# Where PSUM is emptied: 35 reads of PSUM move from VectorE to ScalarE in an adaLN attention and MLP block, with one addition on GpSimd

## The chip, the core and the metric

One core of a Trainium2 chip runs the whole program. The metric is the device time of one execution in microseconds (us); less is better. The engines are called as the profile calls them: PE is TensorE (PEld its weight loads), DVE is VectorE, ACT is ScalarE, POOL is GpSimd, SP is the queue that issues the transfers. Each engine works through its own instructions in the order in which the program lists them.

## What is computed

A transformer block with adaptive layer norm, on 2048 rows of 512 numbers in float32: attention with 32 heads of 16 and a single key and value head, then an MLP of width 1376. The reference, cut to what matters:

```
mod = (silu(c) @ w_mod)                      # six rows: sa, ca, ga, sb, cb, gb
h = layernorm(x) * (1 + ca) + sa
q = h @ wq ; k = h @ wk ; v = h @ wv         # 32 heads for q, one for k and v
p = softmax(q k^T * 16 ** -0.5) ; o = p v
x = x + ga * (o @ wo)
h = layernorm(x) * (1 + cb) + sb
x = x + gb * (gelu(h @ w1 + b1) @ w2 + b2)   # the output
```

## The kernel before

**Units and steps.** The rows are cut into 8 blocks of 256, the heads into 8 groups of 4. A unit is one block with one group (64 units), and it goes over the 2048 keys in 8 steps of 256 keys. The kernel writes all instructions in an order of its own, so each engine's order is what the Python code emits.

**What a step does.** `sexp` makes four products `e` of keys and queries (L589, 64 rows of the array each, 512 columns) and four exponentials from them into `p` (L590, on ACT). `pv` multiplies the `p` of an earlier step with the values (L601, `acc`). `Max.step` makes products `m` for a unit that comes later (L509), from each of which DVE takes the maximum (L514, `mx`). In most steps there is also half of a *batch*: a few products of the other work (query projections `qps`, output projection `wops`, transposes `tp`, first MLP layer `w1ps`, second MLP layer `w2ps`), given out in generators by `batches` and cut in two halves of 64 array rows (L184), one for each of two neighbouring steps. What a generator does behind its last product runs when the second half has been issued (`go_on_`, which calls `resume`).

**PSUM.** The products `e` rotate over three banks, `m` over three, `acc` has one, and all batches share a single bank with the tag `x`. Where two steps hold the halves of a batch, the second one's four `e` take the banks 0, 1, 2 and 0, and when the next step holds a new batch its first `e` takes bank 0 again:

```python
groups = [mixture(maxes(1, n // 2, 0.0), exps(1, [(X, 0, 0), (X, 1, 1), (Y, 0, 2)])),
          halves(batch, 0) + exps(0, [(X, 0, 0)])]
...
issue(mixture(maxes(0, n // 2, 0.0, reduces), exps(0, [(X, 1, 0), (Y, 0, 1), (Y, 1, 2)])),
      halves(batch, 1) + [(0.0, go_on_)] + exps(1, [(Y, 1, 0)]))
```

The last number in each triple is the bank. `go_on_` stands ahead of the step's fourth exponential, so whatever it puts on ACT stands there too.

**The three places that the change touches.** `qproj_late` copies a query sum out of PSUM (L442) and lets POOL split it in a high and a low part; it runs 14 times, early. `modulate` copies the first of two transposed pairs of a block (L862), for POOL to scale; it does so in the 7 blocks whose flag `fast` is not set. `store` adds `x1` to a sum of the second MLP layer (L967) and sends the rows out; there are two sums per block, 14 in those 7 blocks. The eighth block (`fast`, at the end) keeps its code. `later(n, ...)` puts a call off by n ticks of the schedule's clock; two steps take four ticks.

Of the kernel before, what the change touches and what calls it, by code (L numbers as in the profile page):

```python
# [11 lines left out]
ALU = mybir.AluOpType  # L12
# [36 lines left out]
def adaln_mqa_mlp(  # L49
# [15 lines left out]
    nc = tc.nc  # L65
# [60 lines left out]
    def split(dst_h, dst_l, src, eng_h, eng_l, between=None):  # L126
        if eng_h is nc.gpsimd:
            eng_h.tensor_scalar(out=dst_h, in0=src, scalar1=1.0, scalar2=0.0, op0=ALU.mult, op1=ALU.add)
        elif eng_h is nc.scalar:
            eng_h.copy(dst_h, src)  # L130
        else:
            eng_h.tensor_copy(out=dst_h, in_=src)
        if between:
            between()
        eng_l.tensor_tensor(out=dst_l, in0=src, in1=raw(dst_h), op=ALU.subtract)  # L135
# [7 lines left out]
    def later(n, fn):  # L143
        if draining[0]:
            fn()
        else:
            pending.append((clock[0] + n, fn))
# [17 lines left out]
    def batches(ps, pairs, size, ready=lambda n: True, begin=True, end=True):  # L165

        todo = [(a, b_) for wh, wl, xh, xl in pairs for a, b_ in ((wh, xh), (wl, xh), (wh, xl))]
        last = len(todo) - 1
        parts = -(-len(todo) // size)
        for i in range(parts):  # L170
            part = range(i * len(todo) // parts, (i + 1) * len(todo) // parts)
            while not ready(part[-1] // 3):
                yield -1
            yield [(ps, *todo[n], begin and n == 0, end and n == last) for n in part]
# [230 lines left out]
    def send_q(b, g, qH, qL):  # L405
        for t, src in enumerate((qH, qL)):
            nc.sync.dma_start(out=dq[b][g][t].rearrange("a r j n -> (a r j) n"), in_=raw(src))
        state["q"] -= 1
        sent.add((b, g))
# [3 lines left out]
    def qpairs(b, g):  # L413
        hH, hL = hts[b]
        gs = slice(g * P, (g + 1) * P)
        return [(wqH[:, k, gs], wqL[:, k, gs], hH[:, k, :], hL[:, k, :]) for k in range(KD)]

    def qtiles(b, g):
        qH = att.tile([P, BQ], F32R, name=f"qH{b}_{g}", tag="xH", bufs=2)
        qL = att.tile([P, BQ], F32R, name=f"qL{b}_{g}", tag="xL", bufs=2)  # L420
        return qH, qL
# [16 lines left out]
    def qproj_late(b, g):  # L438
        ps = psum.tile([P, BQ], F32, name=f"qps{b}_{g}", tag="x")
        yield from batches(ps, qpairs(b, g), BATCH)  # L440
        q32 = wts_pool["rest"].tile([P, BQ], F32, name=f"q32_{b}_{g}", tag="ot", bufs=2)
        nc.vector.tensor_copy(out=q32, in_=ps)  # L442
        qH, qL = qtiles(b, g)
        split(qH, qL, q32, nc.gpsimd, nc.gpsimd)
        later(4, lambda: send_q(b, g, qH, qL))
# [334 lines left out]
    def rest_steps(b, fast, rp, bank, ons, ready):  # L780
# [4 lines left out]
        for hf in range(w // HQ):  # L785
# [5 lines left out]
            x1, w1ts = early[b]  # L791
# [38 lines left out]
            for t in range(2):  # L830
                ps = psum.tile([P, D], F32, name=f"wops{b}_{hf}_{t}", **bank())
# [27 lines left out]
            def modulate(dp, ps):  # L859
                if not fast and dp == 0:  # L860
                    src = rp.tile([P, 2, HQ], F32, name=f"tc{b}_{hf}", tag="ot", bufs=2)
                    nc.vector.tensor_copy(out=src, in_=ps)  # L862
                for d2 in range(2):
                    d = 2 * dp + d2
                    h32 = rp.tile([P, HQ], F32, name=f"h322_{b}_{hf}_{d}", tag="h322", bufs=2)
                    if fast or dp:
                        nc.scalar.activation(h32, ps[:, d2, :], AF.Identity, scale=cb1[:, d:d + 1], bias=sb[:, d:d + 1])
                    else:
                        nc.gpsimd.tensor_scalar(out=h32, in0=src[:, d2, :], scalar1=cb1[:, d:d + 1], scalar2=sb[:, d:d + 1],
                                                op0=ALU.mult, op1=ALU.add)  # L870
                    if fast:
                        split(hH[:, d, :], hL[:, d, :], h32, nc.vector, nc.gpsimd if d2 else nc.vector)
                    else:
                        split(hH[:, d, :], hL[:, d, :], h32, nc.gpsimd, nc.gpsimd)
# [6 lines left out]
            if fast:  # L881
                tps = [psum.tile([P, 2, HQ], F32, name=f"tp2_{b}_{hf}_{dp}", **bank()) for dp in range(KD // 2)]
                for t in range(2):
                    for dp in range(KD // 2):
                        turn2(dp, tps[dp], t)
                    stir(STIR[t])
                for dp in range(KD // 2):
                    modulate(dp, tps[dp])
                for t in range(2):
                    add_bias(t)  # L890
                yield MOD_WAIT
            else:
                for dp in range(KD // 2):
                    ps = psum.tile([P, 2, HQ], F32, name=f"tp2_{b}_{hf}_{dp}", **bank())
                    yield [(ps[:, d2, t * P:(t + 1) * P], xh[:, t, (2 * dp + d2) * P:(2 * dp + d2 + 1) * P], ident,
                            t + d2 == 0, t + d2 == 2) for t in range(2) for d2 in range(2)]
                    modulate(dp, ps)
                yield 4
# [50 lines left out]
            for f in range(GROUP if fast else 0, NF):  # L949
# [3 lines left out]
                ps = psum.tile([P, HQ], F32, name=f"w1ps{b}_{hf}_{f}", **bank())  # L953
# [10 lines left out]
            def store(t, ps, cols=slice(0, D)):  # L964
                row = row0 + hf * HQ + t * P
                ot = rp.tile([P, D], F32, name=f"ot{b}_{hf}_{t}", tag="ot", bufs=2)
                nc.vector.tensor_tensor(out=ot[:, cols], in0=ps[:, :cols.stop - cols.start], in1=x1[:, t, cols], op=ALU.add)  # L967
                send = lambda: nc.sync.dma_start(out=of[row:row + P, cols], in_=ot[:, cols])
                if fast:
                    send()  # L970
                else:
                    later(2, send)

            while weights:
                yield 2
            for t in range(2):
                sl = slice(t * P, (t + 1) * P)
                for cols in (slice(0, D), ):
                    place = dict(tag="m", bufs=3) if b == len(blocks) - 2 and t else bank()
                    ps = psum.tile([P, D], F32, name=f"w2ps{b}_{hf}_{t}_{cols.start}", **place)  # L980
                    ops = [(gH[:, f, sl], gL[:, f, sl], w2H[:, f, cols], w2L[:, f, cols]) for f in range(NF)]
                    yield from batches(ps[:, :cols.stop - cols.start], ops, BATCH, lambda f: made.issuperset(range(f + 1)))
                    if fast:
                        later(1, lambda t=t, ps=ps, cols=cols: store(t, ps, cols))
                        yield 2
                    else:
                        store(t, ps)
# [158 lines left out]

    draining[0] = True
    late = [qproj_late(b, g) for b in range(2) for g in range(KD)]
    projections = [qproj(b, g) for b in range(2) for g in range(KD)]

# [105 lines left out]
    mod_state["rows"] = wts_pool["rest"].tile([P, D], F32, name="modl_sb", tag="x1", bufs=2)  # L1256
    nc.scalar.copy(mod_state["rows"], mod_state["ps"])
    put_off(*late, late_mods(), *[qproj_late(b, g) for b in range(2, NB) for g in range(KD)])

    steps = [NKT * blocks[b][1] // BQ for b, _ in units]  # L1260
# [169 lines left out]
```

## Time and profile before

| what | value |
|---|---|
| time, median of 3 runs | 1600.91 us (1600.77 to 1601.91) |
| profiled execution: its own time | 1599.49 us |
| profiled execution: span from first to last instruction | 1597.6 us |
| granted TensorE clock, mean over the span | 0.996 of full speed |
| PE busy | 1560.3 us, 98% |
| DVE busy | 1412.9 us, 88%, 2473 instructions |
| ACT busy | 1203.0 us, 75%, 2393 instructions |
| POOL busy | 666.1 us, 42%, 1176 instructions |

The profile is one execution. Busy time is the union of an engine's instructions, and PE's products overlap each other, so a PE that is busy all the time may still be waiting for something between two products; the chain of work that ended last and the order of single instructions tell more.

### The profile page before, as it was taken

What the parts mean: (1) busy time and instruction counts of PE and PEld (TensorE: products, weight loads), DVE (VectorE), ACT (ScalarE), POOL (GpSimd) and SP (SyncE); (2) the same over time, 40 slices, a digit from 0 to 9 for tenths busy, and PEclk for the clock granted to TensorE, in tenths of its full rate; (3) what the DMA queues carried; (4) which work ended last, traced back from release to release, by engine and by line L of the source; (5) the groups of instructions that cost most, each with busy time, mean ns of one, the idle gap of its engine ahead of it and who ended that gap; (6) DMA issues with size and microseconds to landing.
All of it is one profiled execution on the core that took longest, in us unless ns stands there. A gap on an engine that the chain in (4) does not pass through costs nothing.

```text
span 1597.6 us, 41064 instructions
## 1 busy us (share of the span) xinstructions
PE 1560.3 (98%) x16369; PEld 1006.3 (63%) x16369; DVE 1412.9 (88%) x2473; ACT 1203.0 (75%) x2393; POOL 666.1 (42%) x1176
## 2 busy tenths in 40 slices
PE   5999999999999999999999999999999999999998
PEld 3466665557665676657665676656666576656667
DVE  6899999899999998999989999999999999999715
ACT  5577778778777887778877887778877787778853
POOL 4445344747422571246413462234602474225711
PEclk8999999999999999999999999999999999999999
DMA  7136312313022220303112120213112130122232
GB/s 257 73 109 205 117 68 71 125 32 107 17 63 65 68 68 25 103 17 106 32 44 84 53 85 22 78 42 98 42 35 91 42 98 18 62 72 64 80 132 74
DMA packets 79285, 121.59 MB, mean 76 GB/s; under 512 B 15774, under 2 KB 52382, under 8 KB 78836
## 3 DMA queue, kind: packets, MB, share of 16 engines
q1 hardware_dynamic: 79076, 118.95, 23.2%
q8 instruction: 128, 2.10, 0.6%
q14 instruction: 65, 0.53, 0.1%
q10 hardware_dynamic: 16, 0.00, 0.0%
HBM read 91.13 MB, written 27.27 MB: 74 GB/s over the span
## 4 chain that ended last, share of the span: by engine, by line
PE 90%; DVE 6%; DMA 2%; POOL 1%; SPq 1%; ACT 0%; issue 0%; DVEq 0%; POOLq 0%
PE acc L601 30%; PE m L509 22%; PE e L589 17%; PE w1ps L184 8%; DVE mx L514 5%; PE w2ps L184 4%; PE wops L184 2%; PE qps L184 1%; PE w2ps L178 1%; DMA xt<-in_A_x_dram 1%; PE w1ps L178 1%; PE tp L184 1%; PE kps L160 1%; DMA qst<-dq 1%; DVE st L807 0%; DMA os<-drs 0%
## 5 line engine op out<-in xcount | busy, mean ns | idle before, releaser
L514 DVE TENSOR_REDUCE mx<-m 128x1 f32<-128x512 f32 x2048 | 1271.4, 682 | 107.6 <-PE m L509 81.3
L590 ACT ACTIVATE p<-e 128x512 f32<-128x512 f32 x2048 | 1069.4, 599 | 311.1 <-PE e L589 233.2
L509 PE MATMUL m<-ks,qst 64*128 64x512 f32 x2048 | 823.9, 425 | 17.4 <-DVE mx L514 11.0
L589 PE MATMUL e<-qst,ks 64*128 64x512 f32 x2048 | 739.1, 409 | 2.8 <-ACT p L590 1.5
L601 PE MATMUL acc<-p,va 128*32 128x256 f32 x8192 | 550.5, 386 | 0.6 <-DMA qst<-dq 0.6
L509 PEld LDWEIGHTS m<-ks,qst 64*128 64x128 f32 x2048 | 364.1, 184 | 185.8 <-DVE mx L514 157.0
L589 PEld LDWEIGHTS e<-qst,ks 64*128 64x128 f32 x2048 | 366.6, 185 | 85.2 <-ACT p L590 59.5
L601 PEld LDWEIGHTS acc<-p,va 128*32 128x32 f32 x8192 | 214.9, 109 | 220.6 <-issue 115.7
L184 PE MATMUL w1ps<-h2H,w1t 64*128 64x256 f32 x1232 | 236.3, 288 | 0.0
L558 POOL TENSOR_SCALAR mt<-turned 8x32 f32<-8x32 f32 x256 | 53.2, 208 | 362.4 <-DVE turned L564 350.4
L184 PEld LDWEIGHTS w1ps<-h2H,w1t 64*128 64x128 f32 x1232 | 184.2, 185 | 31.7 <-issue 23.0
L184 PE MATMUL w1ps<-h2L,w1t 64*128 64x256 f32 x616 | 169.4, 275 | 0.0
L184 PE MATMUL w2ps<-w2H,gH 64*128 64x512 f32 x286 | 118.1, 413 | 0.0
L184 PE MATMUL w2ps<-w2L,gH 64*128 64x512 f32 x286 | 117.4, 411 | 0.0
L184 PE MATMUL w2ps<-w2H,gL 64*128 64x512 f32 x286 | 117.4, 410 | 0.0
L184 PEld LDWEIGHTS w1ps<-h2L,w1t 64*128 64x128 f32 x616 | 113.8, 185 | 0.0
L920 POOL TENSOR_SCALAR tt<-tt 128x256 f32<-128x256 f32 x77 | 31.1, 404 | 162.8 <-ACT tt L919 162.8
L744 POOL TENSOR_TENSOR os<-os 128x256 f32<-128x256 f32 x28 | 20.6, 734 | 100.9 <-DMA os<-drs 100.2
L921 POOL TENSOR_TENSOR tt<-tt,z 128x256 f32<-128x256 f32 x77 | 57.1, 741 | 6.4
L135 POOL TENSOR_TENSOR gL<-z,gH 128x256 fp32r<-128x256 f32 x77 | 56.8, 738 | 6.4
L931 POOL TENSOR_TENSOR z<-tt,z 128x256 f32<-128x256 f32 x77 | 56.5, 733 | 6.0
L930 POOL TENSOR_TENSOR tt<-tt,z 128x256 f32<-128x256 f32 x77 | 56.7, 736 | 0.0
(188 smaller groups left out, 1498.2 us busy)
## 6 DMA issues: line engine op xcount, KB each, us to landing
w1t<-dw SPq DMA_DIRECT2D x82, 512.0 KB
qst<-dq SPq DMA_DIRECT2D x128, 64.0 KB
do<-oc SPq DMA_DIRECT2D x64, 128.0 KB
dw<-w1s SPq DMA_DIRECT2D x11, 512.0 KB
xt<-in_A_x_dram SPq DMA_DIRECT2D x4, 1024.0 KB
dq<-qH SPq DMA_DIRECT2D x16, 256.0 KB
dq<-qL SPq DMA_DIRECT2D x16, 256.0 KB
qst<-dq SPq DMA_DIRECT2D x128, 32.0 KB
```

Of the source, the lines that this page charges most:

```text
L135: eng_l.tensor_tensor(out=dst_l, in0=src, in1=raw(dst_h), op=ALU.subtract)
L178: nc.tensor.matmul(ps, a, b_, start=first_, stop=last_)
L184: nc.tensor.matmul(ps, a[rows], b_[rows], start=first_ and s == 0, stop=last_ and s == 1)
L509: nc.tensor.matmul(m, qsts[u][rows, j, t * P:(t + 1) * P], ks[rows, kc * 512:(kc + 1) * 512], start=True, stop=True)
L514: nc.vector.tensor_reduce(out=self.mx[u][:, i, kc:kc + 1], in_=m, axis=AX.X, op=ALU.max)
L558: nc.gpsimd.tensor_scalar(out=mt[:, g:g + 32], in0=turned[g:g + 4 * T, :], scalar1=1.0, scalar2=0.0, op0=ALU.mult, op1=ALU.add)
L589: nc.tensor.matmul(e, ks[rows, kt * P:(kt + 1) * P], rhs, start=True, stop=True)
L590: nc.scalar.activation(ptiles[u, K][:, j, s, :], e, AF.Exp, scale=0.25)
L601: ins = nc.tensor.matmul(accs[u][32 * cidx:32 * cidx + 32, :], va[:, kt, :], rhs, start=kt == 0, stop=kt == NKT - 1)
L921: nc.gpsimd.tensor_tensor(out=tt, in0=tt, in1=z, op=ALU.mult)
L930: nc.gpsimd.tensor_tensor(out=tt, in0=tt, in1=z, op=ALU.mult)
L931: nc.gpsimd.tensor_tensor(out=z, in0=tt, in1=z, op=ALU.add)
```

## The change

In `qproj_late` and `modulate` the copy out of PSUM is issued on ACT in place of DVE. In `store` the addition that read PSUM becomes a copy on ACT and, one tick later, an addition in place on POOL; the rows are sent after four ticks in place of two. The last block's `store` is as before.

```diff
@@ qproj_late
         q32 = wts_pool["rest"].tile([P, BQ], F32, name=f"q32_{b}_{g}", tag="ot", bufs=2)
-        nc.vector.tensor_copy(out=q32, in_=ps)
+        nc.scalar.copy(q32, ps)
         qH, qL = qtiles(b, g)
@@ modulate
                 if not fast and dp == 0:
                     src = rp.tile([P, 2, HQ], F32, name=f"tc{b}_{hf}", tag="ot", bufs=2)
-                    nc.vector.tensor_copy(out=src, in_=ps)
+                    nc.scalar.copy(src, ps)
@@ store
                 ot = rp.tile([P, D], F32, name=f"ot{b}_{hf}_{t}", tag="ot", bufs=2)
-                nc.vector.tensor_tensor(out=ot[:, cols], in0=ps[:, :cols.stop - cols.start], in1=x1[:, t, cols], op=ALU.add)
                 send = lambda: nc.sync.dma_start(out=of[row:row + P, cols], in_=ot[:, cols])
                 if fast:
+                    nc.vector.tensor_tensor(out=ot[:, cols], in0=ps[:, :cols.stop - cols.start], in1=x1[:, t, cols], op=ALU.add)
                     send()
                 else:
-                    later(2, send)
+                    nc.scalar.copy(ot[:, cols], ps[:, :cols.stop - cols.start])
+                    later(1, lambda: nc.gpsimd.tensor_tensor(out=ot[:, cols], in0=ot[:, cols], in1=x1[:, t, cols], op=ALU.add))
+                    later(4, send)
```

On ACT, at the end of the first block's first sum of the second MLP layer (`p_7` and `e_7` belong to the last step of a unit, `p_0` and `e_0` to the first step of the next one; in `e_7_1_1` the numbers are step, key half and array half):

```order
 L590 ACTIVATE p_7_6678<-e_7_0_0_6708 128x512
 L590 ACTIVATE p_7_6678<-e_7_1_0_6716 128x512
+L972 COPY ot_0_0_6719<-w2ps_0_0_0_6207 128x512
 L590 ACTIVATE p_7_6678<-e_7_1_1_6723 128x512
 L590 ACTIVATE p_0_6742<-e_0_0_1_6743 128x512
```

The copy stands between the third and the fourth exponential of the step; the other 31 copies that have a batch behind them stand in the same position.

On DVE, at the same place, the instruction that goes:

```order
 L514 TENSOR_REDUCE mx_6483<-m_1_0_0_0_6696 128x1
 L514 TENSOR_REDUCE mx_6483<-m_1_0_1_0_6704 128x1
-L967 TENSOR_TENSOR ot_0_0_6719<-w2ps_0_0_0_6207,x_0_4235 128x512
 L514 TENSOR_REDUCE mx_6483<-m_1_0_2_0_6712 128x1
 L514 TENSOR_REDUCE mx_6483<-m_1_0_3_0_6726 128x1
```

The two maxima behind it stand directly behind the two ahead of it now.

On PE, the first products of the step behind that copy, with what each waits for; first before:

```order
L601 MATMUL acc_6474<-p_6_6659,va 32x256 x3
L184 MATMUL w2ps_0_1_0_6721<-w2H,gH_0_5023 128x512 [waits DVE_49]
L509 MATMUL m_1_1_0_1_6739<-ks,qst_159 128x512
L589 MATMUL e_0_0_1_6743<-qst_158,ks 128x512 [waits Activation_49]
L509 MATMUL m_1_1_1_1_6746<-ks,qst_159 128x512 [waits DVE_49]
```

and with the change:

```order
L601 MATMUL acc_6474<-p_6_6659,va 32x256 x3
L184 MATMUL w2ps_0_1_0_6721<-w2H,gH_0_5023 128x512 [waits Activation_49]
L509 MATMUL m_1_1_0_1_6739<-ks,qst_159 128x512 [waits DVE_49]
L589 MATMUL e_0_0_1_6743<-qst_158,ks 128x512 [waits Activation_49]
L509 MATMUL m_1_1_1_1_6746<-ks,qst_159 128x512 [waits DVE_49]
```

The order is the same. The new batch's first product, which needs bank `x`, waits for ACT in place of DVE, and the step's first `e`, which needs bank 0, waits for ACT in both: for the exponential of `e_7_1_1`.

## Rows read from the trace of the kernel before

**Rows 1.** The page, busy time of each engine (share of the span) and instructions.

```profile
PE 1560.3 (98%) x16369; PEld 1006.3 (63%) x16369; DVE 1412.9 (88%) x2473; ACT 1203.0 (75%) x2393; POOL 666.1 (42%) x1176
```

**Rows 2.** The page, the chain that ended last: shares of the span by engine.

```profile
PE 90%; DVE 6%; DMA 2%; POOL 1%; SPq 1%; ACT 0%; issue 0%; DVEq 0%; POOLq 0%
```

**Rows 3.** The chain in order of time, 440 to 448.5 us: start, us, what.

```profile
444.44 1.00 PE acc L601 x16
447.28 1.01 PE acc L601 x16
```

**Rows 4.** The chain in order of time around the last query copy.

```profile
243.73 1.27 DVE mx L514 x2
245.04 0.69 DVE q L442
245.74 1.21 DVE mx L514 x2
```

**Rows 5.** Lines and tiles: count, duration in ns (min/median/max), first and last start.

```profile
L442 DVE COPY q<-qps x14: 690/692/692, 95.5 to 245.0; 128x512 f32<-128x512 f32 x14
L862 DVE COPY tc<-tp x7: 679/682/682, 335.3 to 1436.2; 128x512 f32<-128x512 f32 x7
L967 DVE TENSOR_TENSOR ot<-w2ps,x x16: 683/692/692, 444.2 to 1593.9; 128x512 f32<-128x512 f32 x16
L433 ACT COPY q<-qps x1: 585/585/585, 70.8 to 70.8; 128x512 f32<-128x512 f32 x1
```

**Rows 6.** Timeline around the w2ps sum that ends at 444.2: start, us, engine, instruction.

```profile
444.76 0.59 ACT L590 ACTIVATE p<-e 128x512 f32<-128x512 f32 x1
...
444.37 1.07 PE L601 MATMUL acc<-p,va 128*32 128x256 f32 x16
...
445.36 0.18 PEld L184 LDWEIGHTS w2ps<-w2H,gH 64*128 64x128 f32 x1 [0.41 <-DVE ot L967]
...
445.48 0.19 PEld L589 LDWEIGHTS e<-qst,ks 64*128 64x128 f32 x1
...
445.70 0.39 PE L589 MATMUL e<-qst,ks 64*128 64x512 f32 x1
...
446.13 2.07 ACT L590 ACTIVATE p<-e 128x512 f32<-128x512 f32 x4 [0.78 <-PE e L589]
```

**Rows 7.** Timeline, the same places after a query copy and a transposed-pair copy.

```profile
106.94 1.08 ACT L590 ACTIVATE p<-e 128x512 f32<-128x512 f32 x2
...
108.14 0.19 PEld L589 LDWEIGHTS e<-qst,ks 64*128 64x128 f32 x1
...
519.36 0.62 ACT L590 ACTIVATE p<-e 128x512 f32<-128x512 f32 x1
...
520.11 0.19 PEld L589 LDWEIGHTS e<-qst,ks 64*128 64x128 f32 x1
```

**Rows 8.** Timeline after two ACT instructions `h` of the second transposed pair.

```profile
525.05 1.04 ACT L867 ACTIVATE h<-tp,sb,cb 128x256 f32<-128x256 f32 x2
...
525.95 0.62 ACT L590 ACTIVATE p<-e 128x512 f32<-128x512 f32 x1
...
526.62 0.49 PE L589 MATMUL e<-qst,ks 64*128 64x512 f32 x1 [0.21 <-ACT p L590]
```

**Rows 9.** Timeline, weight loads later in the step of group 6.

```profile
446.78 0.18 PEld L509 LDWEIGHTS m<-ks,qst 64*128 64x128 f32 x1 [0.19 <-DVE mx L514]
446.78 0.18 PEld L589 LDWEIGHTS e<-qst,ks 64*128 64x128 f32 x1
```

**Rows 10.** Groups by line, form kept apart: busy us, mean ns, idle before.

```profile
L823 POOL TENSOR_TENSOR x<-x,b2g 128x512 f32<-128x512 f32 x16 | 20.1, 1278 | 0.0
```

**Rows 11.** Timeline near the end, around the seventh block's second sum.

```profile
1560.52 0.68 DVE L967 TENSOR_TENSOR ot<-w2ps,x 128x512 f32<-128x512 f32 x1
1561.49 1.02 ACT L867 ACTIVATE h<-tp,sb,cb 128x256 f32<-128x256 f32 x2 [7.41 <-PE tp L879]
```

## The prediction

> **What bounds the kernel now.** I read the page first, then the chain that ended last, then single instructions around the places of the change. The page has PE busy all the time, DVE for 88% and ACT for 75% [rows 1], which invites taking work from DVE. The chain says something else: 90% of the span lies on PE, 6% on DVE, 0% on ACT [rows 2]. In order of time the chain runs from one `acc` to the next at a steady pace, 444.44 to 447.28, which is 2.84 us for a step [rows 3]; DVE comes into it in short pieces only. Of the 35 instructions that leave DVE, one is in the chain: the last query copy, 0.69 us at 245.04 between maxima [rows 4]. So on DVE there is next to nothing to win.
>
> The step of 2.84 us is then looked at for what it waits for. At the end of a step that closes a batch, ACT's fourth exponential runs from 444.76 to 445.35; PE works at `acc` meanwhile, begins the next step with weights at 445.36, and loads the weights of that step's first `e` at 445.48 [rows 6]. This `e` goes into bank 0, which the fourth exponential has just read. The load comes 0.13 us after the exponential's end. It comes 0.12 us after it behind a query copy (106.94 + 1.08 = 108.02, then 108.14) and 0.13 us behind a transposed-pair copy (519.36 + 0.62 = 519.98, then 520.11) [rows 7]; I looked at all 32 such places, and they lie between 0.11 and 0.13 us. How close can it come? Where a first `e` on bank 0 was held in earnest, by an exponential that ended at 525.95 + 0.62 = 526.57, it went at 526.62, 0.05 us later [rows 8]. That leaves 0.06 to 0.08 us of room. ACT is idle for 0.78 us in each step [rows 6], but that idle time lies behind the fourth exponential and ahead of the next step's first one: it waits for this very `e`.
>
> **What is removed.** From DVE: 14 query copies of 0.692, 7 pair copies of 0.682 and 14 of the 16 additions of 0.692 [rows 5], together 24.2 us of DVE's time. What they hold up: the maxima behind them, and through the three `m` banks PE's next `m`. After the addition at 444.24 an `m` does wait for a maximum, 0.19 us until 446.78, but the `e` beside it starts at 446.78 too [rows 9], and that one is set by ACT: the step's first exponential began at 446.13, one takes 0.60 (0.59 and 0.62 in rows 6 and 7), so it ended at 446.73. Taking the DVE part away leaves the step as it is. I cost the removal at 0. The bounds are a gain of 0.69 us, the copy in the chain, and, if those waits for `m` were what counts, 32 x 0.19 = 6.1 us; I take 0 since PE is the one in the chain there [rows 3].
>
> **What is added on ACT.** 35 copies of 128 x 512 out of PSUM. The trace has one on ACT, 0.585 us [rows 5]. Four exponentials of 0.60 in a row took 2.07 us [rows 6], so each behind the first adds (2.07 - 0.60) / 3 = 0.49, 0.11 less than it lasts; a copy among them adds about 0.585 - 0.11 = 0.48. Its data are there in time, since the batch's last product is issued ahead of the third exponential's. The copy stands ahead of the fourth exponential, as the order of ACT in the section on the change shows. So that one ends at 445.35 + 0.48 = 445.83, and the next step's first `e` can load weights at 445.83 + 0.05 = 445.88 in place of 445.48: 0.40 late. PE takes its products in order; it has two products to issue ahead of this `e`, and they go at the old time, so PE then stands idle. A held `e` starts with its weights and takes 0.49 (526.62, rows 8); it would end at 446.37, where it ended at 445.70 + 0.39 = 446.09 before [rows 6]. That is **0.28 us**, and everything behind it in the step follows: the first exponential, the fourth `e` that waits for it, `acc`. The next step has the same small room as ever, so nothing is won back.
>
> The bounds of one copy's price: at most the 0.48 by which ACT is late, plus 0.04 because bank `x` comes free when the copy ends (about 445.35 + 0.05, against 445.36); at least the 0.1 that half of the known case gives, where two ACT instructions of 1.04 us in the same position left PE idle for 0.21 us [rows 8]. That case is milder, because the step behind it holds no batch and uses bank 0 only for a later `e`. I take 0.28, worked out on the kind of step that we have here.
>
> How many are there? Of the 14 query copies 13 have a batch in the next step (95.5 to 233.5; the fourteenth, at 245.0, has none behind it), all 7 pair copies do (the second pair's transposes), and of the 14 sums of the second MLP layer 12 do; the last block but one ends at 1543 without further exponentials. That makes 13 + 7 + 12 = 32, and 32 x 0.28 = **9.0 us**.
>
> **What I cost at nothing.** The three copies without a batch behind them: the fourteenth query copy delays only a later `e` of its step, as the case of rows 8 at half the load, and has DVE's 0.69 of relief against it [rows 4]; of the last two, the second would run on ACT while it is idle, 7.41 us until 1561.49, and the DVE addition that goes there, at 1560.52, was followed by a wait for that ACT work anyway [rows 11]. POOL's 14 additions: a POOL addition of the same size takes 1.28 us [rows 10], 17.9 us in all, on an engine that is busy for 42% [rows 1]. Queued behind them are the gather of turned maxima and the next block's normalisation, which start many microseconds later; without that cover each would cost up to 1.28. The rows are sent two ticks later, and SP's order moves the second send of a block behind four sends of turned maxima, so a late POOL addition can't hold those up; nobody waits for rows on their way out before the end. The consumers of the copies on POOL get their data about 0.4 us later; they had whole steps to spare.
>
> **The sum.** The profiled execution has a span of 1597.6 us and took 1599.49, 1.42 below the median of 1600.91. 1597.6 + 9.0 = 1606.6 of span, 1608.5 for such an execution, and **1609.9 us** beside the median.
>
> **The rivals.** *Hidden* (13%): ACT's idle 0.78 us in a step takes the copy, and PE makes up for the delay inside the step. For it speaks that 0.78 is more than 0.48; against it, that the idle time ends with the very `e` that the copy holds back. It gives 1600.2 to 1602 us.
>
> *DVE's relief counts* (10%), on the other side: PE's steps behind the removed instructions are set by the `m` that waits for a late maximum. Its price is the 0.19 us wait of rows 9 at 32 places, 6.1 us, so 1594.8 us. It decides if the copy costs PE less than 0.19 at a place, that is, if the fourth exponential may be that late unnoticed. Against it: the `e` that starts in the same instant for a reason on ACT. The Trainium skill, Perfetto Trace Analysis, "Optimizing Scalar/DVE Operations", says that where DVE is saturated, offloading some work to Scalar or even GPSIMD may make sense; by that rule this rival would be the likely one, and up to 24.2 us could be won. The trace agrees that DVE is the busier of the two, and does not agree that it is what the steps wait for.
>
> *Dearer* (11%): the whole 0.48 and the 0.04 of bank `x` arrive on PE, since after a stall PE refills both of its halves: 32 x 0.52 = 16.6 us, so 1617.5 us.
>
> My forecast has 66%, and its own range is 32 x 0.1 to 32 x 0.42, 1604 to 1614 us.
>
> **How the numbers follow.** About 0.2%, 3.2 us, is what a measurement of this kernel can tell from no change. Slower by more holds the forecast and the dearer case, 77%; no change is the hidden case, 13%; faster is the third, 10%. The range from 1601 to 1616 leaves out the faster case, part of the hidden one and half of the dearer one, about 2 in 10.
>
> **What would show it.** Right: DVE falls by about 24 us of busy time and ACT rises by about 20; behind each copy one step of the chain takes about 3.1 us in place of 2.84, and the first `e` of that step shows a wait of some 0.3 us on PE for ACT; waits of `e` for ACT grow by about 10 us in total; all other steps keep their pace. The ACT copy itself should last 0.58 to 0.60 us. Wrong: steps of 2.84 us straight through the copies (hidden), or steps behind them that are shorter (relief). What would make the forecast wrong is a first `e` that does not wait for the exponential behind the copy, or slack in PE's step that I have not seen; a stretch far from the copies that changes its pace would mean that POOL or SP, not ACT, made the difference.

## The result and the profile after

The changed kernel takes 1608.57 us (median of 4 runs, 1607.9 to 1608.85) against 1600.84 (4 runs): ratio 1.0049, 95% interval 1.0031 to 1.0066, 7.7 us slower (by the interval, 5.0 to 10.6). The profiled execution after took 1608.57 us with a span of 1606.8, which is 9.2 us above the span of the profiled execution before.

The page of the changed kernel, busy times and the chain by engine, which answer to [rows 1, 2]:

```profile
PE 1569.5 (98%) x16369; PEld 1007.3 (63%) x16369; DVE 1396.7 (87%) x2438; ACT 1219.7 (76%) x2428; POOL 683.7 (43%) x1190
...
PE 90%; DVE 5%; DMA 1%; POOL 1%; ACT 1%; SPq 0%; issue 0%; DVEq 0%; ACTq 0%; POOLq 0%
```

DVE lost 16 us of busy time and the kernel became slower. PE still holds 90% of the chain: what was lost is idle time inside PE's steps, which neither row shows.

Lines of the changed kernel that answer to [rows 5, 10]: count, ns (min/median/max), first and last start.

```profile
L442 ACT COPY q<-qps x14: 580/580/584, 95.9 to 248.8; 128x512 f32<-128x512 f32 x14
L862 ACT COPY tc<-tp x7: 607/607/607, 339.4 to 1444.9; 128x512 f32<-128x512 f32 x7
L972 ACT COPY ot<-w2ps x14: 580/580/607, 448.5 to 1567.3; 128x512 f32<-128x512 f32 x14
L973 POOL TENSOR_TENSOR ot<-ot,x x14: 1269/1282/1289, 449.1 to 1568.5; 128x512 f32<-128x512 f32 x14
```

The chain of the changed kernel at the first sum of the second MLP layer (start, us, what), and the timeline there, which answer to [rows 3, 6]:

```profile
448.16 1.00 PE acc L601 x16
451.26 1.02 PE acc L601 x16
```

```profile
448.09 1.07 PE L601 MATMUL acc<-p,va 128*32 128x256 f32 x16
448.47 0.58 ACT L972 COPY ot<-w2ps 128x512 f32<-128x512 f32 x1
448.93 0.62 ACT L590 ACTIVATE p<-e 128x512 f32<-128x512 f32 x1
449.10 0.18 PEld L184 LDWEIGHTS w2ps<-w2H,gH 64*128 64x128 f32 x1 [0.42 <-ACT ot L972]
...
449.60 0.18 PEld L589 LDWEIGHTS e<-qst,ks 64*128 64x128 f32 x1 [0.32 <-ACT p L590]
449.60 0.50 PE L589 MATMUL e<-qst,ks 64*128 64x512 f32 x1
...
449.67 1.39 DVE L514 TENSOR_REDUCE mx<-m 128x1 f32<-128x512 f32 x2 [0.47 <-PE w2ps L184]
...
450.14 0.60 ACT L590 ACTIVATE p<-e 128x512 f32<-128x512 f32 x1 [0.59 <-PE e L589]
```

Read from the start of `acc`: the new batch's first product loads weights 1.01 us behind it (before 0.99), the first `e` 1.51 behind it (before 1.11). So `e` is 0.40 us late. It loads its weights 0.05 after the end of the fourth exponential, 448.93 + 0.62 = 449.55, and ends 2.01 behind `acc`, where it ended at 1.72: 0.29 lost. The step takes 3.10 us where it took 2.84. DVE sits idle for 0.47 us there: its relief is real and nobody uses it.

With the starts of `acc` compared step by step, the steps behind the 13 query copies are 0.21 to 0.23 us longer (one 0.30), together 3.0; behind the 7 pair copies 0.28 to 0.29, together 2.0; behind the 12 sums 0.27 to 0.31 (one 0.21), together 3.3. That makes 8.3 us. Of the steps one further on, 12 of the 13 behind query copies are 0.02 to 0.07 longer too, together 0.5. Other steps move by up to half a microsecond both ways (five of them are 0.26 to 0.31 shorter) and nearly cancel: the last product of the last `acc` starts 8.48 later. From there to the end another 0.7 goes. The place of 0.6 of it is in the timeline of the changed kernel near the end, which answers to [rows 11], with the same instructions of the kernel before under it:

```profile
1568.47 1.28 POOL L973 TENSOR_TENSOR ot<-ot,x 128x512 f32<-128x512 f32 x1
...
1568.53 1.50 DVE L819 TENSOR_SCALAR xh<-x,mv,rs 128x512 f32<-128x512 f32 x1 [0.46 <-POOL rs L816]
...
1571.51 0.30 PEld L178 LDWEIGHTS w1ps<-h2H,w1t 128*128 128x128 f32 x2 [0.27 <-DVE h2H L132]
```

```profile
1560.06 0.55 DVE L819 TENSOR_SCALAR xh<-x,mv,rs 128x512 f32<-128x512 f32 x1 [0.46 <-POOL rs L816]
...
1562.43 0.30 PEld L178 LDWEIGHTS w1ps<-h2H,w1t 128*128 128x128 f32 x2 [0.27 <-DVE h2H L132]
```

The last block's second normalised half `xh` took 1.50 us in place of 0.55 while the new POOL addition ran beside it, and the first product of the last MLP came 2.98 us behind the start of `xh`, before 2.37. Here nothing else is left for PE to do.

Why a query step loses 0.22 where a sum's loses 0.28 stands in its last weight loads, here behind the third query copy, of the kernel before (with the maximum that ended just ahead) and of the changed kernel:

```profile
120.25 0.68 DVE L514 TENSOR_REDUCE mx<-m 128x1 f32<-128x512 f32 x1
120.91 0.18 PEld L589 LDWEIGHTS e<-qst,ks 64*128 64x128 f32 x1 [0.19 <-ACT p L590]
120.98 0.18 PEld L509 LDWEIGHTS m<-ks,qst 64*128 64x128 f32 x1
```

```profile
121.75 0.18 PEld L589 LDWEIGHTS e<-qst,ks 64*128 64x128 f32 x1 [0.18 <-ACT p L590]
121.76 0.18 PEld L509 LDWEIGHTS m<-ks,qst 64*128 64x128 f32 x1
```

Before, the last `m` went 0.07 behind the fourth `e` and 0.05 behind the end of a maximum (120.25 + 0.68 = 120.93): DVE set the end of this step. So it was in 12 of the 13 query steps, by 0.05 to 0.07, and behind one sum, by 0.09; these are the steps that lose 0.21 to 0.23, and the one query step where `m` went with `e` loses 0.30. With the change both go together. The fourth `e` is 0.28 later here too, 2.69 us behind its `acc` in place of 2.41, but the first 0.06 of that had been lost to DVE already. This also bounds what DVE's relief alone could give in these steps: about 0.06 at each of 13 places, 0.8 in all, since behind the other copies the fourth `e` is as late as the last `m`.

### The profile page after: what moved, and what is told of

The parts are those of the page before. It is cut to its first block, busy times and chain, and to the rows that moved or that the text cites. A ratio compares the mean times of both kernels' runs of the same rounds, so it can differ in the third digit from the quotient of the medians.

```text
span 1606.8 us, 41079 instructions
## 1 busy us (share of the span) xinstructions
PE 1569.5 (98%) x16369; PEld 1007.3 (63%) x16369; DVE 1396.7 (87%) x2438; ACT 1219.7 (76%) x2428; POOL 683.7 (43%) x1190
## 4 chain that ended last, share of the span: by engine, by line
PE 90%; DVE 5%; DMA 1%; POOL 1%; ACT 1%; SPq 0%; issue 0%; DVEq 0%; ACTq 0%; POOLq 0%
PE acc L601 30%; PE m L509 22%; PE e L589 18%; PE w1ps L184 8%; DVE mx L514 4%; PE w2ps L184 4%; PE qps L184 2%; PE w2ps L178 1%; PE wops L184 1%; PE tp L184 1%; PE w1ps L178 1%; PE kps L160 1%; DMA qst<-dq 1%; PE modr L280 0%; DMA wm<-in_w_mod_dram 0%
## 5 line engine op out<-in xcount | busy, mean ns | idle before, releaser
L921 POOL TENSOR_TENSOR tt<-tt,z 128x256 f32<-128x256 f32 x77 | 57.1, 741 | 6.4
L973 POOL TENSOR_TENSOR ot<-ot,x 128x512 f32<-128x512 f32 x14 | 17.9, 1280 | 92.3 <-ACT ot L972 92.3
```

The costliest lines, as they stand in the source:

```text
L921: nc.gpsimd.tensor_tensor(out=tt, in0=tt, in1=z, op=ALU.mult)
```

## The experiments

The theory is *held e*: a copy ahead of the fourth exponential delays the next step's first `e`, which uses the same bank. The rivals are that DVE's work or POOL's addition or the copy itself sets the price. "Before" is timed with each group of runs: 1598.67 us for the banks without the other edits and the work done twice, 1599.14 for the halves in tiles of their own, 1599.01 for the rest.

### Another bank for the first e

```diff
+                if batch[0][3]:
+                    rot[0] = (rot[0] + 1) % 3
+                k0, k1, k2, k3 = four(0)
-                groups = [mixture(maxes(1, n // 2, 0.0), exps(1, [(X, 0, 0), (X, 1, 1), (Y, 0, 2)])),
+                groups = [mixture(maxes(1, n // 2, 0.0), exps(1, [(X, 0, k0), (X, 1, k1), (Y, 0, k2)])),
...
```

Cut to the main lines; `four(0)` gives the banks `rot[0]`, `rot[0] + 1`, `rot[0] + 2` and `rot[0]` again, modulo 3. The step whose batch begins a new sum takes the next bank for its first `e`, and all other `e` follow in turn. This was put into the kernel before:

> The kernel before, but a batch that begins a new sum takes its four e in banks 1, 2, 0, 1 (then 2, 0, 1, 2 for the next sum, and so on), so that the first e of that step no longer goes into the bank that the exponential just ahead of it has read. All three copies stay on VectorE. Theory (the first e is held by the late fourth exponential): without a copy on ScalarE that e has 0.06 us of room, so the choice of bank changes nothing: 1600 to 1601.5 us. Rival (the step is bound by the loop from e over the exponential back to e, copy or no copy): the freed bank shortens steps, up to 32 x 0.1 us, 1597.5 us.

and into the changed kernel:

> The changed kernel with the same choice of banks as in the run before this one: the copies are on ScalarE, ahead of the fourth exponential, but the next step's first e doesn't need that exponential's bank. Theory (held e): the 0.2 to 0.3 us behind each of the 32 copies go, except for some 0.04 us because the shared bank comes free only when the copy ends; with the 0.6 us at the end of the program 1601 to 1603.5 us. Rivals (ScalarE's load as such, or the late release of the shared bank, makes the price): it stays, 1607.5 to 1609 us.

Measured: before with these banks 1596.33 us (11 runs; ratio 0.9987, 0.9978 to 0.9996); changed with these banks 1599.95 (11 runs; 1.0006, 0.9997 to 1.0015), a little under the 1601 to 1603.5 expected. In the first of the two, where no change was expected, the 32 steps kept their length to 0.01 us, so the rival that the freed bank shortens them is out; yet the time is 2.3 us less, and that isn't explained. The timeline of the changed kernel with these banks, at the same place:

```profile
443.42 1.07 PE L601 MATMUL acc<-p,va 128*32 128x256 f32 x16
443.80 0.58 ACT L972 COPY ot<-w2ps 128x512 f32<-128x512 f32 x1
444.26 0.62 ACT L590 ACTIVATE p<-e 128x512 f32<-128x512 f32 x1
...
444.54 0.19 PEld L589 LDWEIGHTS e<-qst,ks 64*128 64x128 f32 x1
...
445.25 1.57 ACT L590 ACTIVATE p<-e 128x512 f32<-128x512 f32 x3 [0.38 <-PE e L589]
```

The copy and the exponential stand as before, but `e` loads its weights while that exponential still runs, 1.12 us behind `acc`, and ACT's idle time ahead of the next step falls from 0.59 to 0.38: now it takes up the copy. The page's row of these weight loads, of the kernel before, changed, and changed with the banks (busy, mean ns, idle before and what ended it):

```profile
L589 PEld LDWEIGHTS e<-qst,ks 64*128 64x128 f32 x2048 | 366.6, 185 | 85.2 <-ACT p L590 59.5
```

```profile
L589 PEld LDWEIGHTS e<-qst,ks 64*128 64x128 f32 x2048 | 365.9, 184 | 95.4 <-ACT p L590 67.1
```

```profile
L589 PEld LDWEIGHTS e<-qst,ks 64*128 64x128 f32 x2048 | 366.2, 184 | 87.7 <-ACT p L590 59.8
```

The waits of `e` for ACT that the change brought are gone, and of 0.21 to 0.31 us a place at most 0.10 is left behind the query copies, pair copies and first sums, and 0.10 to 0.19 behind the second sums: 2.3 of the 8.3 us. Held *e* is shown for the other 6.1, since the same banks alone left these steps as they were. Two things are left. The step's first exponential begins 1.83 us behind `acc` (445.25 - 443.42) where it began at 1.76 (446.13 - 444.37, rows 6); why stays open. And behind a second sum the late release of bank `x` does count:

```profile
478.28 0.58 ACT L972 COPY ot<-w2ps 128x512 f32<-128x512 f32 x1
478.97 0.18 PEld L184 LDWEIGHTS wops<-woH,onH 64*128 64x128 f32 x1 [0.51 <-POOL ml L135]
```

This product goes 0.11 after the copy's end (478.28 + 0.58 = 478.86) and 1.10 behind its `acc`, where it was 1.00 before. The program has PE wait there for this copy, in an instruction ahead of the product; the POOL instruction named ended at about the same time.

With the holds gone, DVE's relief brings no gain that the time shows: the changed kernel is 3.6 us slower than the kernel before with the same banks. Of that the two traces show 2.3 at the 32 places and 0.8 behind the last `acc`.

### The copy twice, and DVE's work twice

```diff
         nc.scalar.copy(q32, ps)
+        nc.scalar.copy(q32, ps)
```

Each of the 35 copies of the changed kernel is issued twice; one of the three places is shown.

> The changed kernel with each of its 35 copies on ScalarE issued twice in a row. Theory (held e): the room is used up by the first copy, so the second one arrives on TensorE whole, 0.45 to 0.49 us at each of 32 places: 1623 to 1625 us. Rival (a stall of TensorE has a fixed price for starting again, whatever its length): 1608 to 1611 us.

Measured: 1628.57 us (4 runs; 1.0189, 1.0173 to 1.0204); 0.83 to 0.93 us a place over before. The timeline:

```profile
455.32 0.58 ACT L974 COPY ot<-w2ps 128x512 f32<-128x512 f32 x1
455.94 0.59 ACT L975 COPY ot<-w2ps 128x512 f32<-128x512 f32 x1
456.42 0.60 ACT L591 ACTIVATE p<-e 128x512 f32<-128x512 f32 x1
...
457.07 0.18 PEld L590 LDWEIGHTS e<-qst,ks 64*128 64x128 f32 x1 [0.32 <-ACT p L591]
```

The exponential starts 0.48 behind the copy ahead of it, but the second copy 0.62 behind the first: it writes the same tile, the program makes it wait for the first, and it began only after that one had ended. So the first `e` came 0.61 later than with one copy (2.12 us behind `acc` against 1.51), not 0.48, and PE paid all of it: here, with the room used up, a late ACT cost its full lateness. The expected mechanism held, its size was off by that spacing.

```diff
+                if not fast:
+                    nc.vector.tensor_tensor(out=ot[:, cols], in0=ps[:, :cols.stop - cols.start], in1=x1[:, t, cols], op=ALU.add)
                 nc.vector.tensor_tensor(out=ot[:, cols], in0=ps[:, :cols.stop - cols.start], in1=x1[:, t, cols], op=ALU.add)
```

The same with DVE's 35 instructions in the kernel before (again one of three places):

> The kernel before with each of its 35 instructions on VectorE issued twice in a row, 24 us more of VectorE's time. Theory (VectorE's part of these places is off the path): 1600.5 to 1602 us. Rival (the maxima behind these instructions hold TensorE's m, and taking the instructions away gave time back): at least the 0.19 us wait again at 32 places, 1607 us, and up to 1625 us if all of it is on the path.

Measured: 1622.67 us (4 runs; 1.0149, 1.0135 to 1.0162), about 0.73 us at all 32 places (one 0.88). My theory missed this. The timeline:

```profile
454.82 0.69 DVE L970 TENSOR_TENSOR ot<-w2ps,x 128x512 f32<-128x512 f32 x1
455.55 0.69 DVE L971 TENSOR_TENSOR ot<-w2ps,x 128x512 f32<-128x512 f32 x1
456.16 2.47 DVE L515 TENSOR_REDUCE mx<-m 128x1 f32<-128x512 f32 x4
...
456.29 0.18 PEld L184 LDWEIGHTS w2ps<-w2H,gH 64*128 64x128 f32 x1 [0.76 <-DVE ot L971]
...
456.89 0.18 PEld L510 LDWEIGHTS m<-ks,qst 64*128 64x128 f32 x1 [0.30 <-DVE mx L515]
```

The second addition starts 0.73 behind the first, for which the program makes it wait too, and PE paid all of that. Bank `x` comes free later, and then every `m` waits for a maximum, DVE running without a gap. So before the change DVE, too, had hardly any room at these places: more work there costs, although less work can bring 0.06 at most, because the `e` is held by ACT nearly as long as the `m` by DVE. "Little to win" did not mean "room to spare".

### Half to each engine

Each copy is cut in two, 256 columns to each engine (one of the three places is shown):

```diff
-        nc.scalar.copy(q32, ps)
+        nc.scalar.copy(q32[:, :HQ], ps[:, :HQ])
+        nc.vector.tensor_copy(out=q32[:, HQ:], in_=ps[:, HQ:])
```

> The changed kernel with each copy cut in two: ScalarE copies the first 256 columns, VectorE the other 256 (in the sums of the second MLP layer too, where GpSimd still adds x1). A copy of 256 columns on ScalarE lasts 0.372 us and so delays the fourth exponential by about 0.26 in place of 0.48. Theory (held e, whose weights may come 0.06 us later for nothing and whose product hides 0.1 us more once it is held): 0.05 to 0.10 us at each of 32 places and the 0.6 us at the end, 2 to 4 us over the kernel before. Rival (a price in proportion to ScalarE's added time): 0.14 us at each place, 5 us over the kernel before.

Measured: 1619.01 us (4 runs; 1.0126, 1.0112 to 1.014), 0.58 to 0.67 us a place. Both theories missed: half a copy on ACT cost more than a whole one. In the trace DVE's half began only 0.03 us after ACT's had ended. To tell whether the shared tile or the shared bank was the reason, the halves got tiles of their own (in the sums DVE adds x itself); then the banks were rotated as well:

```diff
-        nc.scalar.copy(q32, ps)
+        nc.scalar.copy(qa, ps[:, :HQ])
+        nc.vector.tensor_copy(out=qd, in_=ps[:, HQ:])
```

> The halves again, but ACT's 256 columns and DVE's 256 columns go into tiles of their own (for the second-MLP sums DVE adds x directly in its half). In the run with one shared tile DVE's half began 0.03 us behind the end of ACT's, after a wait of 0.89 us with two maxima queued behind it. Theory A: DVE waits because both halves read one PSUM bank, and the program puts one reader behind the other: 0.6 us at 32 places as before, 1615 to 1621 us. Theory B: it waits because both halves write one tile: with own tiles the halves run side by side, ACT is late by 0.37 - 0.11 = 0.26 in place of 0.48, of which the room of 0.06 to 0.08 and the shorter e (0.39 for 0.49) leave about 0.1 us a place, 1600 to 1604 us.

> The halves in tiles of their own, with the banks of e rotated at each new batch. Theory A (one reader of the bank behind the other): the hold of the first e goes, but DVE's wait and the late bank x stay, since the runs with more work on DVE at these places lost 0.6 to 0.7 us there: 1612 to 1620 us. Theory B (the shared tile was the cause): no hold and both engines relieved: 1595.5 to 1599 us, that is the time of the kernel before with the same banks, 1596.3, or up to 1 us less if relief of DVE counts.

Measured: 1625.14 us (4 runs; 1.0163, 1.0139 to 1.0188) and, with the banks, 1624.22 (4 runs; 1.0155, 1.0138 to 1.0171). The timeline with own tiles:

```profile
460.13 0.37 ACT L978 COPY ot<-w2ps 128x256 f32<-128x256 f32 x1
460.38 0.61 ACT L593 ACTIVATE p<-e 128x512 f32<-128x512 f32 x1
460.53 0.42 DVE L979 TENSOR_TENSOR od<-w2ps,x 128x256 f32<-128x256 f32 x1 [0.89 <-ACT ot L978]
...
460.87 3.07 DVE L517 TENSOR_REDUCE mx<-m 128x1 f32<-128x512 f32 x5
461.00 0.18 PEld L184 LDWEIGHTS w2ps<-w2H,gH 64*128 64x128 f32 x1 [0.70 <-DVE od L979]
...
461.60 0.18 PEld L512 LDWEIGHTS m<-ks,qst 64*128 64x128 f32 x1 [0.30 <-DVE mx L517]
```

Theory A held in its mechanism, and both times came out above its range: DVE still waits, 0.89 us, for ACT's read of the other half of the bank, with the maxima queued behind it; bank `x` is late, and then each `m`. Rotated banks don't help against that: 0.6 to 0.7 us a place stays. The extra over the shared tile comes from four query places, which cost 1.9 us each because DVE's half there waits for POOL to be done with the tile's last user:

```profile
its engine sat idle before it (us, times) until:
  ACT qa L443: 9.3, 10
  POOL qL L135: 8.7, 4
```

The wait for the bank stands in the program's order, in this line of DVE's:

```
L979 TENSOR_TENSOR od_0_0_6778<-w2ps_0_0_0_6265,x_0_4291 128x256 [waits PE_49,Activation_49]
```

The Trainium skill, PSUM — Partial Sum Buffer, "PSUM bank collisions raise a hardware error", says that two engines must not be on the same bank and quadrant at once, reads against reads included, and that accesses are to be guarded by semaphores. By that rule such halves may not run side by side. No run here tests it: they never did, since the program makes one wait for the other.

### Only the query copies

```diff
-        nc.vector.tensor_copy(out=q32, in_=ps)
+        nc.scalar.copy(q32, ps)
```

The kernel before with this line alone:

> The kernel before with the query copies alone moved to ScalarE. Theory (a price at each place by itself): 13 x 0.23 = 3.0 us over the kernel before, all of it ahead of 250 us, and nothing at the end of the program. Rival (the price comes from several engines being full in the later blocks): less than 1 us.

Measured: 1602.16 us (11 runs; 1.0019, 1.001 to 1.0028), 3.15 us over before; the 13 steps are 0.21 to 0.24 longer in the trace (one 0.31), and the steps behind pair copies and sums stay as they were (one is 0.06 longer). The price belongs to each place by itself.

### The last addition back on DVE

```diff
-                    later(1, lambda: nc.gpsimd.tensor_tensor(out=ot[:, cols], ...))
+                    eng = nc.vector if b == len(blocks) - 2 and t else nc.gpsimd
+                    later(1, lambda: eng.tensor_tensor(out=ot[:, cols], ...))
```

Operands are cut here. In the changed kernel, and in the changed kernel with rotated banks, the seventh block's second addition runs on DVE, behind `xh`.

> The changed kernel, but the addition of x1 to the seventh block's second sum, which GpSimd makes at 1568.47 us while VectorE normalises the last rows, is made by VectorE behind that normalisation; the copy on ScalarE stays. Theory (the two engines' work on the same memory side by side stretches VectorE's xh from 0.55 to 1.50 us): xh takes 0.55 us again, and from the last group of acc to the first product of w1ps in the last block it is 19.0 us as before the change in place of 19.65; 0.5 to 0.7 us under the changed kernel. Rival (the copy on ScalarE or chance): xh stays at 1.5 us and the distance at 19.6.

> The changed kernel with both prices taken away: the other choice of banks for the step behind a copy, and the addition near the end on VectorE. Theory: what is left is the shared bank that comes free a little later, 0.02 to 0.2 us a place, so 0.3 to 2 us over the kernel before. Rival (with the holds gone, VectorE's 24 us less show as a gain): 3 us or more under the kernel before.

Measured: 1607.6 us (5 runs; 1.0057, 1.0043 to 1.0071) and 1600.28 (11 runs; 1.0009, 1.0001 to 1.0018). The times can't tell 0.6 us; the timeline of the first does:

```profile
1567.11 0.55 DVE L819 TENSOR_SCALAR xh<-x,mv,rs 128x512 f32<-128x512 f32 x1 [0.46 <-POOL rs L816]
...
1567.57 0.69 DVE L974 TENSOR_TENSOR ot<-ot,x 128x512 f32<-128x512 f32 x1
...
1569.49 0.30 PEld L178 LDWEIGHTS w1ps<-h2H,w1t 128*128 128x128 f32 x2 [0.27 <-DVE h2H L132]
```

`xh` takes 0.55 us again and the first product comes 2.38 us behind its start. The POOL addition had stretched it. The second kernel, with both prices taken away, is 1.3 us over the kernel before, inside the 0.3 to 2 expected; the rival, a gain of 3 us or more from DVE's relief, is out.

## Why the prediction was right, and where it was off

- **The hold.** The prediction had `e` 0.40 late and the step 0.28 longer; the trace shows 0.40 and 0.29 at the place it was worked out for. The bound of 0.05 us from the one held `e` of [rows 8] carried it. The fourth `e` is 0.28 late in the query steps as well, but 12 of them lose only 0.21 to 0.23, because DVE had set their end about 0.06 later than ACT.
- **The count.** 32 places were named, and these 32 got longer: 8.3 us against 9.0. So nothing was hidden, and the dearer case, 0.52 a place, did not come either.
- **The removal.** It was costed at 0, from one step behind a sum. At 13 of the 32 places the last `m` did go later than the fourth `e`, for DVE, so the removal could be worth up to about 0.8 us, an estimate from the weight loads, against the 6.1 of the rival. With the holds gone no gain showed, so that rival, and the rule beside it, do not apply here. The removal without a copy on ACT was not run. The doubled DVE work shows that the reason I gave was half of it: PE's step was bound by DVE about as closely as by ACT.
- **What was costed at nothing.** This step failed: of POOL's 14 additions I looked only at what queues behind them, not at what DVE does meanwhile. The last one runs beside `xh` with PE waiting, and that made 0.6 us, on top of the sum. Near the end I also took the wait for ACT as cover; it was `xh` that ACT waited for.
- **The sum.** 8.3 at the 32 places, 0.5 in the steps behind query steps and 0.6 at `xh` make 9.4, against a span 9.2 longer; small differences elsewhere make up the rest. The span and the time of the profiled execution, 1606.8 and 1608.57, are those forecast, 1606.6 and 1608.5; the median came out 1.3 us under 1609.9, because the profiled execution before lay 1.4 us under its median and the one after lies on it. Part of the hit is thus luck: what was too high, the query steps, and what was left out, the steps behind them and the end, cancelled.
- **The signs.** Waits of `e` for ACT rose by 7.6 us (10 forecast). Busy time changed by -16.2 on DVE and +16.7 on ACT, where I had -24 and +20: the durations alone add up to 24.1 less on DVE and 21.1 more on ACT, but busy time is a union, and neighbours overlap: on DVE by up to 0.09 us, on ACT by 0.10 to 0.14 around a copy.

The version with rotated banks and without the change is the fastest, 1596.33 us, 0.13% under before. Its trace shows no place where that is won, but the execution traced took 1598.95, 2.6 us over that median, so the gain need not be in it. The cause stays open.

## What to carry to other kernels

Before moving work to an engine with idle time, look at what that idle time waits for: if it ends with a product that this engine itself releases, there may be next to no room: here a copy that made `e` 0.40 us late cost 0.21 to 0.31 at every place, and a second one its whole 0.61. Look at the instruction next in line on that engine and at the PSUM bank it frees; giving the product behind it another bank took three quarters of the price away here. And an engine that has little to win need not have room to lose: check both signs, by taking work away and by doubling it.

## What the hardware showed that I had not expected

- A DVE instruction from SBUF to SBUF took 1.50 us in place of 0.55 beside a POOL addition that began 0.06 us ahead of it and lasted 1.28; without the addition it took 0.55. With rotated banks the same pair gave 1.50 again. The Trainium skill, SBUF — State Buffer, "SBUF: two separate sides", says that GpSimd and some DVE forms share a pair of ports as an exclusive lock, held for a whole instruction. The trace agrees in kind; it lost 0.95 us where waiting out the addition fully would have been 1.22.
- A second ACT copy that the program makes wait for the first starts 0.61 to 0.64 us after it, 0.03 behind its end, while the exponential behind a copy starts 0.46 to 0.48 after it, before the copy has ended. So doubling an instruction in this way overstates what a second, independent one would cost.
